# A transformer layer on one core: whole banks for the probabilities, norm scales on VectorE, four more tiles turned by DMA

## The chip, the cores and the metric

The kernel runs on one core of a Trainium2 chip. The metric is the device time of one execution in microseconds, as the median of several. The engines are named as in the profile: PE (TensorE's matmuls) with PEld (its weight loads), DVE (VectorE), ACT (ScalarE), POOL (GpSimd), and SP (SyncE, which issues nearly all DMA transfers here).

## The reference

One pre-norm layer in float32: an attention over a sliding window of 256 tokens, then a gated feed-forward network.

```python
S, D, H, Dh, W, F = 2048, 448, 16, 28, 256, 1792
def A(x):
    q, k, v = split(x @ wqkv)                       # 16 heads of 28
    s = einsum("hqd,hkd->hqk", q, k) * Dh ** -0.5
    s = where((i - j >= 0) & (i - j < W), s, -1e9)  # causal, 256 wide
    return einsum("hqk,hkd->hqd", softmax(s), v).merge_heads() @ wo
def B(x):
    return (gelu_tanh(x @ w_gate) * (x @ w_up)) @ w_down
h  = x + A(layernorm(x))        # (x - mean) / sqrt(var + 1e-5)
h2 = h + B(layernorm(h))
```

## The kernel before

**Precision.** A float32 product is made of products of a rounded "hi" part and a remainder "lo". ACT writes the hi part with a copy (line 452, `to_hi`), DVE or POOL subtract it from the value for the lo part (line 455, `to_lo`). So every operand of a large product costs one ACT and one DVE or POOL instruction beside the matmuls.

**Tiles.** The 2048 tokens are 16 tiles of 128, which make four chunks of 512 tokens. The 16 heads are four groups of four. A block `B` is a chunk and a group; there are 16 blocks.

**The norms.** `layer_norms` (469) takes one or two tiles. DVE forms mean and variance (`bn_stats` 488, `bn_aggr` 490, into `bnmv`); POOL makes the scales `bnve` in up to four instructions: eps is added (476), the power -0.5 taken (477), the product with the mean formed (483), and the sign turned (484). `normalise` (501) then lets ACT write the normed tile `xn` (511). What follows needs the tile transposed. For most tiles of the first norm PE does that with four transposes (516), and ACT and DVE write hi and lo out of the bank. For the tiles in `TURNED` (12 to 15), and for the second norm, `turn` lets DVE transpose 32x32 squares (556), sends them by four DMA transfers on SP to a buffer `xl` (559), and `turned` fetches them back with two transfers into `xT` (568, 570), from where ACT and DVE make hi and lo.

**Attention.** Projections (672 for values, 710 for queries and keys) write banks of PSUM; SP moves rows of queries and keys to their places (720, `k<-k` and `k<-q`, and 723). Scores are formed twice. First queries by keys (819, `bank<-k,q`, a "score fill"): DVE takes each row's maximum (883) into `mx`, transposes it into `mt` (916), and SP writes it as one more row of the queries (921, `q<-mt`). Then keys by queries with that row (819, `bank<-q,k`, 29 rows, a "probability fill"): ACT takes the exponential into `pp` (889), POOL cuts the mask out (895), PE multiplies with the values (971). The drain (1009 on DVE, with an ACT copy ahead) adds two banks and frees one of them; transposes (1010), a reciprocal (1011), products on POOL (996) and the output product (1036) follow, and DVE adds the result to the residual `hres` (1039).

Both kinds of fills work on tiles of 64x64, four banks at a time, 512 columns in each. The columns come from pieces of a block in units of 64. `filled` puts the pieces one after the other and cuts a piece that crosses the end of a bank; a fill has one matmul for each piece, head and half. `excursion` (797) issues a score fill and the probability fill of an earlier block together.

**The feed-forward part.** Seven pairs of weights. The first three are classical products (1284, 1296), the last four use sums of the operands to save products (1497); the down products are 1573, their additions to `hres` 1593 (`out_add`), the last ones 1609. Sums of tokens are made at 1192, 1195 and 1198, sums of weights at 1356, each by DVE or POOL. Sums of results are taken out of banks at 1503, 1504 and 1509. Where a bank is read by nothing else before PE may write it again, a one-element read (`seen`, 1410 on ACT, 1411 on DVE) stands for that.

**What sets the order.** Nothing is ordered by hand. Each operation is given an engine, a cost, a latency, a key and its dependences, and a list scheduler (`Lists.run`, 185) walks time while the program is built: at each step it takes, on the engine that can start first, the operation with the lowest key among those that can start. `PLACE` adds an offset to the keys of named units. Operations with `alts` (one-element reads, weight and token sums, copies) go to the engine that would end first. Each engine runs its instructions in the order in which they were written, so any change of a cost, key or dependence may move everything behind it. The matmuls of the feed-forward part are in a fixed chain.

Of the kernel before, what the change touches and what calls it, by code (L numbers as in the profile page):

```python
# [11 lines left out]
AF = mybir.ActivationFunctionType  # L12
# [74 lines left out]
TURNED = (12, 13, 14, 15)  # L87
# [24 lines left out]
}  # L112

# [22 lines left out]
class Lists:  # L136
# [3 lines left out]
    def __init__(self):  # L140
        self.ops, self.seen, self.open, self.all, self.unit = [], {}, {}, {}, None
# [172 lines left out]
def block_kernel(ctx: ExitStack, tc, x, wqk_in, wv_in, wo_in, gu_in, rest_in, cw_in, down_in, out):  # L314
# [154 lines left out]
    def layer_norms(ts, key, kind):  # L469
# [4 lines left out]
        def ve():  # L474
# [3 lines left out]
            if quick:  # L478
                return
# [1462 lines left out]
```

## Time and profile before

| | |
|---|---|
| median of 3 runs | 687.98 us (687.2 to 688.15) |
| profiled execution | 688.24 us, its span 686.5 us |
| PE busy | 673.7 us, 98% of the span |
| DVE / ACT / POOL busy | 77% / 53% / 32% |
| chain that ended last | PE L1497 22%, PE L1573 14% |

A row of the timeline has the start, the duration, the engine, the line, the operation, the result and its operands, the tile, and how many instructions it stands for; what is in brackets at its end is the idle time of that engine just before it, and what ended that. Rows of one engine overlap, since the next matmul begins before the last has left the array: the distance between two starts is what counts. SPq rows are transfers being issued. A row of a window has the busy time of each engine in it, with the instructions in brackets, then the granted clock of PE.

### The profile page before, as it was taken

What the parts mean: (1) busy time and instruction counts of PE and PEld (TensorE: products, weight loads), DVE (VectorE), ACT (ScalarE), POOL (GpSimd) and SP (SyncE); (2) the same over time, 40 slices, a digit from 0 to 9 for tenths busy, and PEclk for the clock granted to TensorE, in tenths of its full rate; (3) what the DMA queues carried; (4) which work ended last, traced back from release to release, by engine and by line L of the source; (5) the groups of instructions that cost most, each with busy time, mean ns of one, the idle gap of its engine ahead of it and who ended that gap; (6) DMA issues with size and microseconds to landing.
All of it is one profiled execution on the core that took longest, in us unless ns stands there. A gap on an engine that the chain in (4) does not pass through costs nothing. (4 is left out here: it accounts for less than half of the span.)

```text
span 686.5 us, 22714 instructions
## 1 busy us (share of the span) xinstructions
PE 673.7 (98%) x9097; PEld 564.5 (82%) x9097; DVE 526.9 (77%) x1569; ACT 361.7 (53%) x785; POOL 218.2 (32%) x444
## 2 busy tenths in 40 slices
PE   8999999999999999999999999999999999999997
PEld 7877778778877776788877988888889889999886
DVE  8887788787788897169977899767657878877754
ACT  5567656565475555557544474534534545546430
POOL 6245654575555564830501013100001220210000
PEclk9999999999999999999999999999999999999999
DMA  8212121013022363126754875315004644543102
GB/s 309 75 51 48 37 50 36 10 48 69 13 82 61 82 215 112 53 83 156 146 124 108 218 213 149 110 46 162 30 16 131 213 136 134 137 148 87 43 15 108
DMA packets 67082, 69.70 MB, mean 102 GB/s; under 512 B 42528, under 2 KB 55008, under 8 KB 66400
## 3 DMA queue, kind: packets, MB, share of 16 engines
q1 hardware_dynamic: 66832, 68.13, 35.5%
q8 instruction: 71, 1.16, 0.7%
q14 instruction: 35, 0.29, 0.2%
q10 hardware_dynamic: 144, 0.11, 0.0%
HBM read 58.82 MB, written 22.45 MB: 118 GB/s over the span
## 5 line engine op out<-in xcount | busy, mean ns | idle before, releaser
L883 DVE CUSTOM_DVE_ANT_0 mt<-bank,mt 128x192 bf16<-128x192 f32 (+4 forms) x368 | 115.5, 373 | 24.2 <-PE bank L819 23.4
L1497 PE MATMUL bank<-xT,proj 64*128 64x512 f32 x645 | 120.3, 388 | 0.0
L895 POOL TENSOR_SCALAR_AFFINE_SELECT pp<-pp 64x256 f32<-64x256 f32 x240 | 95.3, 415 | 46.9 <-ACT pp L889 41.7
L1497 PE MATMUL bank<-xo,proj 64*128 64x512 f32 x456 | 98.0, 388 | 1.4 <-DVE raw L1509 1.0
L889 ACT ACTIVATE pp<-bank 128x512 f32<-128x512 f32 x152 | 79.4, 599 | 25.2 <-PE bank L819 25.1
L1497 PEld LDWEIGHTS bank<-xT,proj 64*128 64x128 f32 x645 | 81.4, 184 | 8.2
L710 PE MATMUL bank<-xT 128*128 128x512 f32 x308 | 79.6, 402 | 0.1
L1573 PE MATMUL bank<-proj,gh 64*128 64x448 f32 x624 | 74.9, 363 | 0.0
L710 PEld LDWEIGHTS bank<-xT 128*128 128x128 f32 x308 | 55.4, 188 | 15.2 <-ACT pp L889 2.0
L1573 PEld LDWEIGHTS bank<-proj,gh 64*128 64x128 f32 x624 | 62.6, 184 | 6.5 <-ACT e L1410 0.6
L1497 PEld LDWEIGHTS bank<-xo,proj 64*128 64x128 f32 x456 | 60.0, 184 | 7.8 <-DVE raw L1509 1.4
L1497 PE MATMUL bank<-xT,w 64*128 64x512 f32 x276 | 53.6, 389 | 0.0
L1497 PE MATMUL bank<-xo,w 64*128 64x512 f32 x240 | 49.5, 391 | 1.2 <-ACT v L1503 0.9
L819 PE MATMUL bank<-k,q 28*64 28x320 f32 (+4 forms) x1560 | 47.8, 336 | 0.4 <-DVE raw L1009 0.2
L1593 DVE TENSOR_TENSOR hres<-bank,hres 128x448 f32<-128x448 f32 (+1 forms) x85 | 46.9, 608 | 1.0 <-PE bank L1573 1.0
L819 PE MATMUL bank<-q,k 29*64 29x192 f32 (+4 forms) x1664 | 44.6, 328 | 1.4 <-issue 1.4
L819 PEld LDWEIGHTS bank<-q,k 29*64 29x64 f32 x1664 | 30.0, 131 | 17.8 <-issue 10.7
L672 PE MATMUL bank<-proj,xT 128*128 128x448 f32 (+1 forms) x220 | 43.0, 338 | 0.3 <-ACT proj L452 0.3
L1410 ACT ACTIVATE e<-bank 1x1 f32<-1x1 f32 x78 | 12.3, 157 | 54.2 <-PE bank L1573 41.1
L819 PEld LDWEIGHTS bank<-k,q 28*64 28x64 f32 x1560 | 36.0, 131 | 5.2 <-issue 1.5
L672 PEld LDWEIGHTS bank<-proj,xT 128*128 128x128 f32 x220 | 34.8, 189 | 6.2 <-issue 1.8
L1573 PE MATMUL bank<-proj,xT 64*128 64x448 f32 x312 | 38.0, 364 | 1.6 <-DVE e L1411 1.4
(201 smaller groups left out, 1327.7 us busy)
## 6 DMA issues: line engine op xcount, KB each, us to landing
gu<-in_gu_dram SPq DMA_DIRECT2D x18, 480.0 KB
proj<-gu SPq DMA_DIRECT2D x24, 288.0 KB
proj<-down SPq DMA_DIRECT2D x22, 224.0 KB
proj<-gu SPq DMA_DIRECT2D x24, 192.0 KB
hres<-in_x_dram SPq DMA_DIRECT2D x16, 224.0 KB
w<-gu SPq DMA_DIRECT2D x12, 288.0 KB
out_dram<-hres SPq DMA_DIRECT2D x15, 224.0 KB
xT<-xn SPq DMA_DIRECT2D x26, 128.0 KB
```

Of the source, the lines that this page charges most:

```text
L672: op("pe", mm(224 * n), 0.29 if n == 1 else 0.38, key + a / 16, lambda a=a, h=h, wb=wb, xb=xb: nc.tensor.matmul(bank[b.k][:, 0:224 * n], x ...
L710: op("pe", mm(512) + 0.002, 0.403, key, lambda a=a, h=h, wb=wb, xb=xb: nc.tensor.matmul(bank[b.k], wqk[m][:, h, wb, :], xT[:, xb, cc * 128 ...
L819: nc.tensor.matmul(bank[banks[j].k][dst, at:at + 64 * n], w, x, start=True, stop=True, tile_position=(32 * j, 64 * h), skip_group_check=True)
L883: nc.vector.tensor_tensor_reduce(junk[turn_of[0]][:, 0:x], bank[b.k][:, 64 * o:64 * o + x], mask[:, lo:lo + x], 1.0, -BIG, OP.add, OP.max, ...
L889: op("act", 0.065 + width * 0.00088, 0.16 + width * 0.00088, key, lambda: nc.scalar.activation(pp[:, j, at:at + width], bank[b.k][:, 0:wid ...
L895: nc.gpsimd.affine_select(a, a, pattern=[[0, 4], [-cm, 64]], compare_op=op_, fill=0.0, base=0, channel_multiplier=cm)
L1410: ways = {"act": (0.08, 0.17, lambda: nc.scalar.activation(e8[0:1, 0:1], bank[b.k][0:1, 0:1], AF.Copy), False), "dve": (0.07, 0.17, lambda ...
L1497: nc.tensor.matmul(bank[b.k], w, xarea(u.cp, xl, xs, side)[:, xk], start=p in (1, 2, 5) and not k and not t, stop=t == 2, tile_position=(6 ...
L1573: nc.tensor.matmul(bank[banks[q].k][:, 0:D], h[oh][0]()[HALF[x], q * 128:q * 128 + 128], d[wh][0]()[HALF[x]], start=not ph and not y and n ...
L1593: op("dve", 0.07 + w * 0.463 / D, 0.163 + w * 0.463 / D, key, lambda: nc.vector.tensor_tensor(hres[:, t, c0:c0 + w], bank[b.k][:, c0:c0 + ...
```

## The change

- Tiles 8 to 11 of the first norm join `TURNED`: 16 PE transposes go, and four DVE transposes, 16 transfers to DRAM and 8 back come.
- The pieces of the probabilities are laid in another order in blocks from 4 on, and the score tiles of the third chunk too (for the first three groups), so that fewer are cut at a bank's end. Matmuls of the probabilities: 832 before, 736 now; products with the values: 96 fewer; of the scores: 780 before, 772 now. The columns stay as they were.
- The scales of a norm: the eps is added on DVE (for the first four tiles on POOL), the power is taken on POOL, and the negative product with the mean is one DVE instruction that reads POOL's result.
- Of the last down products, the odd quarters of the chunk that is finished last but one are added by an ACT copy into SBUF and a POOL addition instead of a DVE addition.
- The scheduler's cost of a fill grows by 0.03 for each matmul above 23, a case without a choice is caught, operations get names and may be pinned (`HAND`, empty), and `PLACE` has other entries throughout.

```diff
-TURNED = (12, 13, 14, 15)
+TURNED = (8, 9, 10, 11, 12, 13, 14, 15)
...
 PLACE = {
-    "k3": -17.1, "kv0": -31, "ln1.4": 18, "q0.0": 6, "kv1": -72, "v3.0": 77, "ln1.5n": 25, "q0.2": -37, "ln1.10": -54,
+    "k6": 16, "ln1.1": 11, "k1": 24, "ln1.2n": -10, "v1.0": 42, "ln1.4": -36, "q0.0": -108, "kv1": -9, "q0.1": -10,
...
-        def ve():
-            e = bnve[:, :, i:i + n]
-            nc.gpsimd.tensor_scalar(e[:, 0], bnmv[:, i:i + n, 1], EPS, None, op0=OP.add)
-            nc.gpsimd.tensor_tensor(e[:, 1], e[:, 0], nhalf[:, 0:n], op=OP.pow)
-            if quick:
-                return
...
-                nc.gpsimd.tensor_tensor(e[:, 0], bnmv[:, i:i + n, 0], e[:, 1], op=OP.mult)
-                nc.gpsimd.tensor_scalar(e[:, 2], e[:, 0], -1.0, None, op0=OP.mult)
...
+        first = kind == "ln1" and ts[0] < 4
+        cost = 0.3 if first else 0.08
+        op("pool" if first else "dve", cost, cost + 0.09, key(ts[0]), lambda: (nc.gpsimd if first else nc.vector).tensor_scalar(
+            e[:, 0], bnmv[:, i:i + n, 1], EPS, None, op0=OP.add), stats, scales)
+        op("pool", 0.6 + 0.1 * n, 0.65 + 0.1 * n, key(ts[0]), lambda: nc.gpsimd.tensor_tensor(
+            e[:, 1], e[:, 0], nhalf[:, 0:n], op=OP.pow), [*scales, "nhalf"], scales)
+        if not quick:
+            op("dve", 0.08, 0.17, key(ts[0]), lambda: nc.vector.scalar_tensor_tensor(
+                e[:, 2], bnmv[:, i:i + n, 0], -1.0, e[:, 1], op0=OP.mult, op1=OP.mult), [*stats, *scales], scales)
...
-    score_fills = filled([((B, i), len(tile_keys(B, i)[0][0])) for B in range(NB) for i in range(4)])
+    score_fills = filled([((B, i), len(tile_keys(B, i)[0][0])) for B in range(NB)
+                           for i in ((0, 2, 3, 1) if block(B)[1] == 2 and block(B)[0] < NG - 1 else range(4))])
     prob_fills = filled([((B, x), PIECES[x][4]) for B in range(NB) for x in
-                         ("ABdf" if B < 4 else "ABDFCE" if B % 2 == 0 else "CEABDF")])
+                         ("ABdf" if B < 4 else "ACBFED" if B % 2 == 0 else "DACBFE")])
...
-            cost = width * 4 / 2400 + (0.06 if not n and len(steps) > 1 else 0.02)
+            cost = width * 4 / 2400 + (0.06 if not n and len(steps) > 1 else 0.02) + 0.03 * max(0, len(work) - 23)
...
+        aside_ = m == 13 and c and q % 2
+        if aside_:
+            buf, tok = ((VM[6][0], VM[6][1]), (SPARE[2][0], SPARE[2][1]))[q // 2]
+            op("act", 0.47, 0.57, key, lambda: nc.scalar.activation(buf()[:, 0:D], bank[b.k][:, 0:D], AF.Copy), (), [tok], b)
+            op("pool", 1.1, 1.15, key, lambda: nc.gpsimd.tensor_tensor(hres[:, t, :], hres[:, t, :], buf()[:, 0:D], op=OP.add),
+               [h, tok], [h], port=True)
```

The order that results is shown at three places. A row has the line, the operation, the result with its operands, and the tile; line numbers are those of each kernel's own file, where 455 has become 470, 1195 and 1198 have become 1207 and 1210, 1356 is now 1368, 1411 is now 1423, 1509 is now 1521, 559 is now 570, 720 is now 731 and 921 is now 933. The banks 140 to 147 of before are called 144 to 151 after.

First, DVE's queue in the feed-forward part, at the third pair of weights (`w` and `xn` hold a pair's sums of weights). Before:

```order
L1195 TENSOR_TENSOR raw<-raw,xT 64x512
L1356 TENSOR_TENSOR xn<-w_5069,xn 64x384
L1356 TENSOR_TENSOR xn<-w_5069 64x128
L455 TENSOR_TENSOR w_5069<-w_5069 128x384
L455 TENSOR_TENSOR w_5069<-w_5069 128x256
L455 TENSOR_TENSOR w_5069<-xn,w_5069 128x384
L1411 COPY e_74<-bank_145 1x1
```

Now:

```order
L1204 TENSOR_TENSOR raw<-xT 128x512
L1368 TENSOR_TENSOR xn<-w_4865,xn 64x384
L1368 TENSOR_TENSOR xn<-w_4865 64x128
L1423 COPY e_74<-bank_149 1x1
L470 TENSOR_TENSOR w_4865<-w_4865 128x384
L1423 COPY e_74<-bank_151 1x1
L470 TENSOR_TENSOR w_4865<-w_4865 128x256
L470 TENSOR_TENSOR w_4865<-xn,w_4865 128x384
```

The read of the bank (145, now 149) has moved ahead of the three subtractions that write `w`.

Second, DVE's queue where the sums of tokens for the second half are made (`xo`, `xT`, `v`, `e` are buffers of such sums). Before:

```order
L455 TENSOR_TENSOR proj<-proj 128x448
L1192 TENSOR_TENSOR e_5070<-xo 128x512
L1195 TENSOR_TENSOR v<-e_5070,xo 64x512
L455 TENSOR_TENSOR xo<-e_5070,xT 128x512
L455 TENSOR_TENSOR xo<-v,xT 128x512
L1198 TENSOR_TENSOR v<-xT,v 64x512
L1509 TENSOR_TENSOR raw<-bank_141,raw 128x512
L1509 TENSOR_TENSOR e_5071<-bank_143,e_5071 128x512
```

Now:

```order
L470 TENSOR_TENSOR proj<-proj 128x448
L1204 TENSOR_TENSOR e_4866<-xo 128x512
L1207 TENSOR_TENSOR v<-e_4866,xo 64x512
L470 TENSOR_TENSOR xo<-e_4866,xT 128x512
L1521 TENSOR_TENSOR raw<-bank_145,raw 128x512
L1521 TENSOR_TENSOR e_4867<-bank_147,e_4867 128x512
```

The sum of line 1198 is no longer in DVE's queue here, it stands in POOL's, and the subtraction of `v` has moved behind the two reads of banks.

Third, SP's queue around the first row of maxima (`q<-mt`; `xl` and `xT<-xl` are the transfers of turned tiles). Before:

```order
L720 DMA k_157<-q_161 4x512
L1057 DMA raw<-in_wo_dram 128x448
L720 DMA k_157<-q_161 4x512 x3
L921 DMA q_158<-mt 1x4x128 x4
L1057 DMA raw<-in_wo_dram 128x448
L559 DMA xl_136<-xn 32x14x32 x3
L921 DMA q_159<-mt 1x4x128 x4
```

Now:

```order
L570 DMA xl_137<-xn 32x14x32 x4
L731 DMA k_161<-q_165 4x512 x4
L1069 DMA raw<-in_wo_dram 128x448
L579 DMA xT<-xl_137 128x3x128
L581 DMA xT<-xl_137 128x128
L731 DMA k_161<-k_160 4x512
L933 DMA q_162<-mt 1x4x128 x4
L731 DMA k_161<-k_160 4x512 x3
L579 DMA xT<-xl_136 128x3x128
L581 DMA xT<-xl_136 128x128
L1069 DMA raw<-in_wo_dram 128x448
L933 DMA q_163<-mt 1x4x128 x4
```

Transfers of two turned tiles now stand ahead of the first rows of maxima, and the fetch of another between the first and the second.

More of the change, by code (lines that the diff above doesn't have):

```diff
@@ L124 @@
 class Op:
-    __slots__ = ("eng", "cost", "lat", "key", "fn", "deps", "users", "left", "banks", "port", "ready", "start", "fin", "unit",
+    __slots__ = ("eng", "cost", "lat", "key", "fn", "deps", "users", "left", "banks", "port", "ready", "start", "fin", "unit", "name",
                  "size", "tag", "mode", "alts", "then", "soft")
@@ L256, in run @@
                     best = c, e
+            best = best or (choice("pe", False), "pe")
             t, o, got = best[0]
@@ L472, in layer_norms @@
         quick = kind == "ln1" and ts[0] < QUICK
[L474 to L484 removed]
+        e = bnve[:, :, i:i + n]
+        stats, scales = [("bnmv", t % 4) for t in ts], [("bnve", t % 4) for t in ts]
         L.unit = f"{kind}.{ts[0]}"
@@ L491, in layer_norms @@
                [("bnst", t % 2)], [("bnmv", t % 4)])
-        cost = (1.25 if n == 1 else 1.6) - 0.3 * quick
-        op("pool", cost, cost + 0.05, key(ts[0]), ve,
-           [*(("bnmv", t % 4) for t in ts), "nhalf"], [("bnve", t % 4) for t in ts])
+        first = kind == "ln1" and ts[0] < 4
[7 more added lines that the diff above has]
+                e[:, 2], bnmv[:, i:i + n, 0], -1.0, e[:, 1], op0=OP.mult, op1=OP.mult), [*stats, *scales], scales)
         for t in ts:
@@ L1592, in out_add @@
         h = span("h", t + part[0], w / D)
-        op("dve", 0.07 + w * 0.463 / D, 0.163 + w * 0.463 / D, key, lambda: nc.vector.tensor_tensor(
-            hres[:, t, c0:c0 + w], bank[b.k][:, c0:c0 + w], hres[:, t, c0:c0 + w], op=OP.add), [h], [h], b, part=part)
+        aside_ = m == 13 and c and q % 2
[4 more added lines that the diff above has]
+               [h, tok], [h], port=True)
+        else:
+            op("dve", 0.07 + w * 0.463 / D, 0.163 + w * 0.463 / D, key, lambda: nc.vector.tensor_tensor(
+                hres[:, t, c0:c0 + w], bank[b.k][:, c0:c0 + w], hres[:, t, c0:c0 + w], op=OP.add), [h], [h], b, part=part)
         if ORDER2[m][1] not in [c for _, c in ORDER2[m + 1:]]:
```

18 lines of the change are left out of this document (12 added, 6 removed), and 31 rows, old and new, of the table PLACE.

## The prediction

> **What bounds the kernel now.** I read the page's busy shares first, then the windows, the waits of the matmul engine, and the timeline at each wait.
>
> ```profile
> span 686.5 us, 22714 instructions
> PE 673.7 (98%) x9097; PEld 564.5 (82%) x9097; DVE 526.9 (77%) x1569; ACT 361.7 (53%) x785; POOL 218.2 (32%) x444
> ```
>
> PE is idle for only 12.8 us. A change can therefore gain in two ways: shorten PE's own stream, or close a share of these 12.8 us. The windows (columns: us, then busy us of PE, PEld, DVE, ACT and POOL, then the clock) show where the gaps lie and that the clock is full:
>
> ```profile
> 20.00:50.00 30.00, 30.00 (x304) 24.50 (x303) 25.47 (x112) 18.11 (x35) 10.84 (x24) 1.00 0.21 60
> 300.00:350.00 50.00, 48.59 (x500) 40.10 (x486) 46.07 (x89) 33.89 (x75) 12.19 (x13) 1.00 0.54 117
> 400.00:450.00 50.00, 48.27 (x433) 40.68 (x431) 44.41 (x83) 29.24 (x66) 10.07 (x8) 1.00 0.46 136
> 450.00:500.00 50.00, 50.00 (x462) 43.12 (x460) 32.52 (x65) 21.80 (x47) 1.99 (x3) 1.00 0.28 81
> ```
>
> Where DVE is 65% busy (450 to 500) PE never stops; where it is 89 to 92% busy PE loses 1.4 and 1.7 us in 50. So PE bounds the span and DVE's queue makes the gaps. The waits of PE agree (total, times, longest):
>
> ```profile
> PE bank L819 <- issue: 1.6, 2, 1.4
> PE bank L1573 <- DVE e L1411: 1.4, 1, 1.4
> PE bank L1497 <- DVE raw L1509: 1.3, 2, 1.0
> PE bank L1497 <- ACT v L1503: 0.9, 1, 0.9
> ```
>
> The profiled execution took 688.24 us: 686.5 of span and 1.74 around it. The median shown is 687.98, 0.26 lower. I sum against 686.5 and then add 1.74 and take off 0.26.
>
> **Term 1, the transposes.** Tiles 8 to 11 no longer go through PE. Four matmuls fall away for each, priced by the distance from their row to the next on PE:
>
> ```profile
> 29.94 0.60 PE L516 MATMUL bank<-ident,xn 128*128 128x128 f32 x4
> 30.30 0.57 PE L672 MATMUL bank<-proj,xT 128*128 128x224 f32 x3
> ```
>
> 0.36 us for a tile, four tiles: **-1.5 us**, certain if what replaces them is in time (term 7).
>
> **Term 2, the pieces of the scores and probabilities.** The probabilities' matmuls fall from 832 to 736: six fills of 32 become fills of 16 with the same 512 columns in each bank. The scores' fall from 780 to 772: three fills of 32, three of 24, one of 20 and two of 16 become eight of 24 and one of 20. The trace counts two records for each matmul. The first three rows are probabilities, the others scores:
>
> ```profile
> 53.39 1.12 PE L819 MATMUL bank<-q,k 29*64 29x128 f32 x48
> 282.34 1.31 PE L819 MATMUL bank<-q,k 29*64 29x192 f32 x64
> 285.85 1.12 PE L819 MATMUL bank<-q,k 29*64 29x320 f32 x32
> 54.30 1.15 PE L819 MATMUL bank<-k,q 28*64 28x192 f32 x32
> 198.44 1.33 PE L819 MATMUL bank<-k,q 28*64 28x64 f32 x48
> 160.32 1.52 PE L819 MATMUL bank<-k,q 28*64 28x64 f32 x64
> ```
>
> Between 64 and 32 records a fill of probabilities gains 1.31 - 1.12 = 0.19 us: six give 1.1 at most. Where a score fill follows at once it overlaps the end, and the gain may be nothing, so I take **-0.5** (0 to -1.1). The score fills go from 3 x 1.52 + 3 x 1.33 + 2 x 1.15 = 10.85 to 8 x 1.33 = 10.64, the one of 20 left out on both sides; the three full fills could by overlap count for as much as 0.37 each, so I take **-0.5** (-0.2 to -1.1). The products with the values lose as many matmuls, 96. Priced like the 32 extra records above (0.19/32 = 6 ns a record) 192 records are 1.1 us; if columns alone count, nothing. I take **-0.3**, near the low end, since these run as long streams in which each matmul can hide the one before.
>
> The Trainium skill (TensorE: Matmul & The Clock Gate, "Wait — 56ns, not 53.3ns?") says that matmuls never start closer than about 25 ns. Taken for each record, the 400 that go would be worth 10 us, an estimate from that page. The trace disagrees for records: the 48 at 53.39 took 0.91 us to the next row at 54.30, 19 ns each.
>
> **Term 3, the gaps of the second half.** Two are named by the waits. First DVE, then the matmul that waited:
>
> ```profile
> 342.00 0.64 DVE L1195 TENSOR_TENSOR raw<-raw,xT 64x512 f32<-64x512 f32 x1
> 343.46 0.90 DVE L455 TENSOR_TENSOR w<-w 128x384 fp32r<-128x384 f32 x2
> 344.27 0.55 DVE L455 TENSOR_TENSOR w<-xn,w 128x384 fp32r<-128x384 f32 x1
> 344.73 0.14 DVE L1411 COPY e<-bank 1x1 f32<-1x1 f32 x1
> 344.93 1.54 PE L1573 MATMUL bank<-proj,xT 64*128 64x448 f32 x12 [1.38 <-DVE e L1411]
> ```
>
> The one-element read frees a bank, and stood behind the three `w` subtractions. In the changed order it stands ahead of all three, so it can run at about 343.4, 1.3 us earlier: **-1.4**. What is late next are the `w` pieces, weights of a later pair, with more than 1.5 us of PE's stream before them.
>
> ```profile
> 444.66 1.30 POOL L455 TENSOR_TENSOR xo<-xo,xT 128x512 fp32r<-128x512 f32 x1 [8.70 <-ACT xT L452]
> 444.70 1.80 DVE L1198 TENSOR_TENSOR v<-xT,v 64x512 f32<-64x512 f32 x1
> 446.43 0.68 DVE L1509 TENSOR_TENSOR raw<-bank,raw 128x512 f32<-128x512 f32 x1
> 447.16 0.73 PE L1497 MATMUL bank<-xo,proj 64*128 64x512 f32 x3 [1.04 <-DVE raw L1509]
> 401.07 0.68 DVE L1198 TENSOR_TENSOR v<-xT,v 64x512 f32<-64x512 f32 x1
> ```
>
> L1198 took 1.80 us beside a POOL instruction, 0.68 without it. It now goes to POOL and leaves DVE's queue at this place, so L1509 can start some 1.8 us earlier: **-1.0**. What is late next is `v` itself, which ACT rounds into `xT` (L452), for a fill further on. Two gaps of a few tenths follow queues that are shorter in the changed order (near 410 and 417): **-0.5**. Together **-2.9**. The bounds are 0, if new queues cost as much elsewhere, and -6.0, what this part exceeds its steady pitch by.
>
> **Term 4, the gaps of the attention part.** The longest is this one; the three rows ahead of the drain L1009, which frees the bank, are a norm's statistics and two weight subtractions:
>
> ```profile
> 266.16 0.63 DVE L488 BATCH_NORM_STATS2 bnst<-hres 128x6 f32<-128x448 f32 x1
> 266.70 1.15 DVE L455 TENSOR_TENSOR proj<-proj 128x448 fp32r<-128x448 f32 x2
> 267.78 0.68 DVE L1009 TENSOR_TENSOR raw<-bank,oblk 128x512 f32<-128x512 f32 x1
> 268.74 0.45 PE L819 MATMUL bank<-q,k 29*64 29x128 f32 x8 [1.39 <-issue]
> ```
>
> Such meetings are chance of the order. The fills are cut anew and all else is placed anew, so some go and some come: **-1.0**, between 0 and the -4.2 that five such places of this part come to.
>
> **Term 5, the end.** Nine additions follow each other on DVE after the last matmuls begin:
>
> ```profile
> 678.69 4.41 DVE L1593 TENSOR_TENSOR hres<-bank,hres 128x448 f32<-128x448 f32 x9 [0.45 <-PE bank L1573]
> 679.20 2.78 PE L1609 MATMUL bank<-w,gh 128*128 128x448 f32 x15
> ```
>
> PE ends at 681.98, DVE at 683.10, 0.49 us an addition. Two now go by an ACT copy and a POOL addition. Seven leave DVE tied to PE: 681.98 + 0.5 = 682.5, **-0.6**. If POOL's pair of additions (about 1.3 each by the POOL row at 444.66) ends last, nothing is gained; if POOL holds DVE up as at 444.70, it is +0.5. The Trainium skill (SBUF — State Buffer, "Who interferes with whom") has it that VectorE with two SBUF inputs collides with a GpSimd that reads SBUF, with one not. The row at 444.70 agrees for two; these additions read one bank and one SBUF tile, so by the page -0.6 stands.
>
> **Term 6, the scales of the norms.** The reciprocal root stays on POOL, with the eps ahead of it (but for the first tiles) and the last product after it on DVE. DVE now waits for POOL at 16 places:
>
> ```profile
> L477 POOL TENSOR_TENSOR bnve<-bnve 128x2 f32<-128x2 f32 (+1 forms) x17 | 12.7, 747 | 12.7 <-ACT xn L511 11.4
> L895 POOL TENSOR_SCALAR_AFFINE_SELECT pp<-pp 64x256 f32<-64x256 f32 x240 | 95.3, 415 | 46.9 <-ACT pp L889 41.7
> ```
>
> Some eight of the places lie before about 50 us. At the others one or two instructions stand between, 0.1 to 1.3 us against 0.75 (two roots: 1.5) and whatever masks POOL still has, at 0.42 each. Behind the waiting product stand score maxima and bank drains, for which PE waits. Below: nothing. Above: two roots and three masks, 2.7 us, at nine places. I take +0.6 of PE. POOL also loses two instructions a norm, which brings scales earlier. With what other new meetings bring: **+1.0**.
>
> **Term 7, SP's queue.** Tiles 8 to 11 add 16 transfers of transposed rows and 8 back. The prices of an issue are a quarter of each row:
>
> ```profile
> 26.45 2.46 SPq L720 DMA_DIRECT2D k<-k  x4
> 48.13 2.45 SPq L921 DMA_DIRECT2D q<-mt  x4
> 68.42 1.95 SPq L559 DMA_DIRECT2D xl<-xn  x4
> ```
>
> Ahead of the first `q<-mt` (row maxima, without which the first probabilities can't run) now stand 8 `xl` and 2 `xT` more and 4 key copies fewer: 10 x 0.49 - 4 x 0.61 = 2.5 us. It ended at 50.6 and PE used it at 53.39; PE's own work before that point is 1.7 us shorter by the new order and term 1. SP is idle 3.4 us in pieces before 48. So the first fill is late by 2.5 + 1.7 - 2.8 = 1.4 if the idle time can't be used, less if it can; 3.5 if a landing takes as long as the whole slack. I take **+1.0** (0 to 3.5). By the fifth `q<-mt` 16 more issues are 7.8 us, against some 8.8 us of idle.
>
> **Sum.** -1.5 - 0.5 - 0.5 - 0.3 - 2.9 - 1.0 - 0.6 + 1.0 + 1.0 = -5.3. 686.5 - 5.3 + 1.74 - 0.26 = **682.7 us**.
>
> **The rivals.**
>
> *The gaps only move.* PE keeps the fixed terms 1 and 2 (-2.8) and term 5 (-0.6), terms 3 and 4 come back elsewhere, one of the two waits bites (+1): 687.98 - 2.4 = 685.6. For it: DVE is 89 to 92% busy just where the gaps are, and the sum of its work is not smaller. Against it: the two named waits have a single instruction each ahead of them, which the new order moves.
>
> *SP's queue holds the first probabilities* for the whole 3.5 us and again once or twice: the term is +4.7 instead of +1: 686.4. For it: SP issues for nearly all of 22 to 50 us. Against it: later `q<-mt` have margin.
>
> *DVE stands waiting for POOL's root* (slower). Of nine places in the attention part and the first weights each holds the drain or maximum behind it for its 1.5 to 2.7 us, as the two subtractions did at 266.70, where PE lost 1.4. At nine times 0.9, PE loses 8.1 instead of 1: 682.7 + 7.1 = 689.8. It decides when more than 0.7 us a place reaches PE. For it: POOL is the busiest in just this part, and pairs of roots stand together. Against it: PE holds several banks ahead, and most waits of DVE pass unseen.
>
> *Small matmuls cost by number.* At 38 ns a matmul (0.91/24), the 200 that go are worth 7.6 us instead of 1.3: 676.4. Against it: the fill of 64 records took 0.19 us more than that of 32, 12 ns a matmul.
>
> **How the numbers follow.** Forecast 0.50, its own range 679.5 to 685.0; gaps only move 0.18; SP 0.12; DVE waits for POOL 0.13; cost by number 0.07. Less than 0.2%, 1.4 us, can't be told from no change here. Faster: 0.50, two thirds of 0.18, half of 0.12, and 0.07: 0.75. Same: what is left of these two, 0.12. Slower: 0.13. The range leaves out the last two rivals, 0.20: 678.8 to 687.3.
>
> **What would show it.** L516 with 32 records of PE instead of 48; no L819 group over 48 records. Term 3: no wait of PE for the one-element read near 340 nor for `raw` near 445. Term 6: DVE's idle time ahead of the scale product, by POOL, under 1 us a place. Term 7: the idle time of PE before the first probabilities, 0 to 1.5 us. Term 5: the last DVE addition within 0.6 us of PE's end. The prediction is wrong if PE's idle time is not some 2 us smaller, or if its busy time falls by clearly more or less than 2 to 4 us.

## The result and the profile after

The changed kernel takes **679.66 us** (678.54 to 680.05, 4 runs), the kernel before 687.59 us beside it (4 runs): a ratio of 0.9883 with an interval of 0.9866 to 0.9901, 8.0 us faster. The prediction was 682.7 us, 5.3 under the 687.98 it started from. The direction and the range held, the range narrowly: the lower end of the forecast's own range was 679.5. The gain was half as large again as forecast.

The page of after, its first lines:

```profile
span 678.2 us, 21918 instructions
PE 668.4 (99%) x8685; PEld 555.9 (82%) x8685; DVE 531.4 (78%) x1613; ACT 362.9 (54%) x790; POOL 203.3 (30%) x394
```

PE's idle time fell from 12.8 to 9.8 us and its busy time by 5.3 us. The waits of PE in after (total, times, longest):

```profile
PE bank L1890 <- DVE bank L639: 1.6, 1, 1.6
PE bank L527 <- ACT xn L522: 1.0, 1, 1.0
PE bank L1509 <- DVE e L1423: 0.5, 2, 0.4
```

None of the four waits that the prediction quoted is left at over 0.5 us. The windows of after (the same columns as before):

```profile
20.00:50.00 30.00, 30.00 (x299) 24.64 (x299) 25.98 (x124) 17.75 (x35) 6.56 (x8) 1.00 0.33 83
300.00:350.00 50.00, 50.00 (x428) 43.25 (x426) 45.81 (x96) 30.24 (x63) 11.71 (x10) 1.00 0.63 153
350.00:400.00 50.00, 49.46 (x448) 44.48 (x446) 40.57 (x84) 26.29 (x61) 8.23 (x8) 1.00 0.65 169
400.00:450.00 50.00, 50.00 (x456) 42.19 (x456) 40.96 (x76) 26.52 (x59) 7.74 (x7) 1.00 0.40 117
```

From 300 to 350 DVE is as busy as before (45.81 against 46.07), yet PE loses nothing there. So it is not a lighter load of DVE that closed the gaps.

Busy time alone does not say where the 8.3 us of span went, because a short wait hides inside it. A row of before shows this: the ten matmuls behind the wait start 0.53 us after the two ahead of them, which last 0.36, and only 0.17 counts as idle. These twelve take 1.67 us until the next group starts at 412.03, while twelve of the same kind take 1.22 at 414.11 (the next group starts at 415.33): 0.45 us are lost, and 0.17 of them are shown.

```profile
410.36 0.36 PE L1573 MATMUL bank<-proj,xT 64*128 64x448 f32 x2
410.89 1.30 PE L1573 MATMUL bank<-proj,xT 64*128 64x448 f32 x10 [0.17 <-DVE xT L455]
```

So I cut the span at two places that both kernels have on PE: the start of the first group of 42 classical products that has no projections or attention behind it, and the start of the last 15 matmuls. First the timeline of before, whose last 15 start at 679.20, as the prediction shows:

```profile
330.17 1.08 PE L1284 MATMUL bank<-xT,proj 64*128 64x512 f32 x8
```

Then that of after:

```profile
325.66 1.09 PE L1296 MATMUL bank<-xT,proj 64*128 64x512 f32 x8
670.37 1.88 PE L1628 MATMUL bank<-w,gh 128*128 128x448 f32 x8
```

| part of the span | before | after | difference | forecast |
|---|---|---|---|---|
| to the 42 products: norms, attention, first weights | 330.2 | 325.7 | -4.5 | -1.8 (terms 1, 2, 4, 6, 7) |
| from there to the last 15 matmuls | 349.0 | 344.7 | -4.3 | -2.9 (term 3) |
| from there to the end | 7.3 | 7.8 | +0.5 | -0.6 (term 5) |

Each column is one execution. Three kernels further down have before's order in the first part (`pins`, `pins2`, `pins3`), and there it took 328.5 to 330.1 us; three have after's (`no_aside`, `tail`, `scales_pool`), 325.5 to 325.6. The first row's difference is therefore 2.8 to 4.6 us, 3.8 between the means. The second row holds within a few tenths in all of them, but for what the edits there do on purpose.

The windows of the first two parts tell busy from idle time. Before, then after:

```profile
0.00:330.17 330.17, 326.01 (x5945) 257.14 (x5947) 257.42 (x1041) 198.67 (x420) 171.65 (x392) 1.00 0.31 85
330.17:679.20 349.03, 344.89 (x3141) 304.98 (x3137) 265.61 (x521) 163.04 (x366) 46.52 (x53) 1.00 0.41 114
0.00:325.66 325.66, 321.48 (x5532) 247.88 (x5534) 262.08 (x1075) 199.15 (x423) 165.14 (x354) 1.00 0.34 91
325.66:670.37 344.71, 344.17 (x3141) 305.57 (x3137) 266.10 (x533) 163.17 (x368) 35.86 (x38) 1.00 0.42 116
```

In the first part PE's idle time is 4.2 us in both kernels, and its busy time fell by 4.5 us. In the second part its idle time fell from 4.1 to 0.5 us, while DVE's work there stayed the same (265.6 and 266.1 us).

In the second part the groups of matmuls come in the same order in both kernels, so the gain can be followed from group to group. The lead of after is the difference of the two starts, less the 4.51 us that it already had at the 42 products:

| group starts, before | the same group, after | lead of after | what PE waited for on the way, before |
|---|---|---|---|
| 346.31 | 340.41 | 1.4 | one-element read on DVE, at 344.93 |
| 373.49 | 366.62 | 2.4 | `v` of ACT, at 373.49 |
| 423.04 | 415.70 | 2.8 | short waits for DVE, at 410.89 and 418.97 |
| 447.16 | 438.65 | 4.0 | `raw` of DVE, at 447.16 |
| 679.20 | 670.37 | 4.3 | |

The row of the wait for ACT, in before:

```profile
373.49 0.50 PE L1497 MATMUL bank<-xo,w 64*128 64x512 f32 x2 [0.86 <-ACT v L1503]
```

### The profile page after: what moved, and what is told of

The parts are those of the page before. It is cut to its first block, busy times and chain, and to the rows that moved or that the text cites. A ratio compares the mean times of both kernels' runs of the same rounds, so it can differ in the third digit from the quotient of the medians.

```text
span 678.2 us, 21918 instructions
## 1 busy us (share of the span) xinstructions
PE 668.4 (99%) x8685; PEld 555.9 (82%) x8685; DVE 531.4 (78%) x1613; ACT 362.9 (54%) x790; POOL 203.3 (30%) x394
## 4 chain that ended last, share of the span: by engine, by line
PE 88%; DVE 5%; DMA 3%; issue 1%; SPq 1%; ACT 1%; POOL 0%; DVEq 0%; ACTq 0%
PE bank L1509 26%; PE bank L1585 18%; PE bank L831 10%; PE bank L721 9%; PE bank L1296 7%; PE bank L1048 6%; PE bank L983 6%; PE bank L683 4%; PE bank L1308 2%; DVE mt L895 2%; DMA raw<-in_wo_dram 1%; DMA proj<-gu 1%; DMA hres<-in_x_dram 1%; DVE xn L1368 1%; SPq L731 1%
## 5 line engine op out<-in xcount | busy, mean ns | idle before, releaser
L1509 PE MATMUL bank<-xT,proj 64*128 64x512 f32 x645 | 115.6, 389 | 0.0
L1509 PE MATMUL bank<-xo,proj 64*128 64x512 f32 x456 | 92.7, 389 | 0.4 <-DVE e L1423 0.4
L1509 PEld LDWEIGHTS bank<-xT,proj 64*128 64x128 f32 x645 | 73.0, 184 | 9.5 <-ACT raw L1515 0.3
L1585 PE MATMUL bank<-proj,gh 64*128 64x448 f32 x624 | 72.1, 362 | 0.0
L1509 PEld LDWEIGHTS bank<-xo,proj 64*128 64x128 f32 x456 | 55.7, 184 | 6.1 <-DVE e L1423 0.7
L1509 PE MATMUL bank<-xT,w 64*128 64x512 f32 x276 | 50.9, 389 | 0.0
L1509 PE MATMUL bank<-xo,w 64*128 64x512 f32 x240 | 46.4, 390 | 0.2 <-DVE e L1423 0.2
L831 PE MATMUL bank<-q,k 29*64 29x320 f32 (+4 forms) x1472 | 43.7, 350 | 0.2 <-issue 0.2
L831 PEld LDWEIGHTS bank<-q,k 29*64 29x64 f32 x1472 | 27.1, 131 | 18.2 <-issue 7.6
L983 PE MATMUL bank<-pp,v 64*29 64x192 f32 (+4 forms) x1472 | 38.6, 340 | 0.2 <-ACT pp L901 0.2
L1296 PE MATMUL bank<-xT,proj 64*128 64x512 f32 x312 | 37.9, 390 | 0.0
```

The costliest lines, as they stand in the source:

```text
L831: nc.tensor.matmul(bank[banks[j].k][dst, at:at + 64 * n], w, x, start=True, stop=True, tile_position=(32 * j, 64 * h), skip_group_check=True)
L983: nc.tensor.matmul(bank[banks[h].k][32 * j:32 * j + DH + 1, 64 * lo:64 * hi], v[HALF[h], at_v(4 * c - 2 + kh // 2), 4 * g + j, :], pp[HALF ...
L1296: nc.tensor.matmul(bank[banks[side ^ ph].k], cwbuf[n % 4][0]()[HALF[side], o:o + 128], carea(c, xl, j, side), start=not ph and not j and n ...
L1509: nc.tensor.matmul(bank[b.k], w, xarea(u.cp, xl, xs, side)[:, xk], start=p in (1, 2, 5) and not k and not t, stop=t == 2, tile_position=(6 ...
L1585: nc.tensor.matmul(bank[banks[q].k][:, 0:D], h[oh][0]()[HALF[x], q * 128:q * 128 + 128], d[wh][0]()[HALF[x]], start=not ph and not y and n ...
```

## The experiments

Where a number is compared with after, it is by the ratio to the kernel before, which ran beside each: after has 0.9883.

**Do small matmuls cost by number?** `split_d` cuts one piece of the probabilities in two, in the fills and in the products with the values, and keeps every queue's order (a further edit, left out here, leaves the scheduler's costs as they were).

```diff
+    def cut(kh, n):
+        return [(0, n // 2), (n // 2, n - n // 2)] if kh in (8, 3) and n == 4 else [(0, n)]
...
             if probs:
-                return [(j, dst, at, n, keys_of(B, kh, 1)[rows], q_of(B)[rows, 64 * u:64 * (u + n)], h)]
+                return [(j, dst, at + 64 * a, b, keys_of(B, kh, 1)[rows], q_of(B)[rows, 64 * (u + a):64 * (u + a + b)], h)
+                        for a, b in cut(kh, n)]
...
-                        work.append((h, j, kh, lo, u + n, G.at + at + 64 * (lo - u)))
+                        work += [(h, j, kh, lo + a, lo + a + b, G.at + at + 64 * (lo + a - u)) for a, b in cut(kh, u + n - lo)]
```

> The changed kernel with one piece of each block from 4 on (four units wide) cut in two, in the probability fills and in the products with the values: the numbers of matmuls are those of before again (832 and 96 more), the columns and every engine's order stay as after. By the rows of before (64 records 1.31 us, 32 records 1.12): six fills grow by 0 to 0.19 us each and the value products not at all, since their 112 records of before and 96 records of after both take 2.4 to 2.5 us: +0.2 to +1.1, about 680.2. By the theory that small matmuls cost by number (38 ns each, 192 of them): +7.3, about 687.

Measured: 684.42 us, ratio 0.9945 (0.9930 to 0.9960), 4.3 us slower than after. That fits neither number. Two things were wrong with the edit: it added 224 matmuls, not 192, since the piece exists in the first four blocks too, and it put the two halves directly behind each other on the same 64x64 tile.

`split_all` does it with every piece over one unit (`if n > 1` in `cut`):

> The changed kernel with every piece wider than one unit cut in two, in the probability fills and in the value products; columns and order as after. It shows from which number on a fill is bound by its matmuls. By the rows of before nothing is lost up to 48 records and some 0.2 us for each 16 beyond: fills of 64 to 96 records go from 0.92 to 1.1 to 1.6 us, about +10 to +20 us in all with the value products. If columns alone count: +0. If every matmul costs 38 ns: over +40.

Measured: 721.42 us (a single run), 42 more for 1264 more matmuls, twice the most that its rows of before gave. It has the same flaw. It tells only that far smaller pieces would be dear.

`split_d2` mends both, in the fills as shown and in the products with the values alike:

```diff
+    def cut(B, ke, n):
+        return [(0, n // 2), (n // 2, n - n // 2)] if ke == 8 and n == 4 and B > 3 else [(0, n)]
...
-                for j in range(4):
-                    for h, kh, u in ((0, ke, ue), (1, ko, uo)):
-                        work += part(B, h, j, kh, u, n, 64 * o, True)
+                for a, b in cut(B, ke, n):
+                    for j in range(4):
+                        for h, kh, u in ((0, ke, ue), (1, ko, uo)):
+                            work += part(B, h, j, kh, u + a, b, 64 * (o + a), True)
```

> As split_d, but the cut pieces follow each other as whole pieces (in split_d two halves of a piece stood directly behind each other on the same 64x64 tile, and four more blocks were cut), so that the matmuls number 832 and 832 as before, 192 more than after, over the same columns and in the same orders. Term 2 of the prediction: 0.2 to 1.1 us slower than after. By number at the 21 ns that split_d paid for each: 4.1 us slower, 683.7. If split_d's cost came from the order on the tile alone: under 1.5 us.

Measured: 681.49 us, ratio 0.9902 (0.9886 to 0.9918). That is 1.3 us slower than after by the two ratios, whose intervals overlap, and 0.8 in the trace (its first part took 326.4 us). Term 2's 0.2 to 1.1 is the nearest; the 7 us of the rival by number are out, and 4.1 too. An added matmul costs some 7 ns here (1.3 us by 192) and 19 in `split_d`, where consecutive ones share a tile. PE's busy time in the probability fills says the same: 43.7 us in after, 44.6 in `split_d2`, 48.0 in `split_d`.

**Are the two gaps of the second half a matter of DVE's queue?** `pins` is the kernel before, with the pinning of after (`HAND`) and two entries in it: the read of bank 145 and the sum of tokens.

```diff
+HAND = {"None#5": "act", "tx1.0#3": "pool"}
```

> The kernel before with two operations pinned: the one-element read at 344.7 us goes to ACT instead of DVE, the sum of tokens at 444.7 us to POOL instead of DVE; all else is as before. If the two gaps come from DVE's queue as term 3 has it: -1.4 and -1.0, about 685.3, and no wait of PE over 0.5 us near 345 and 447. If gaps only move: the two places are empty but PE waits elsewhere as long, 687.3 or more.

Measured: ratio 0.9989 (0.9976 to 1.0002), no change that can be told. The gap at 447 had shrunk from 1.04 to 0.30, that at 345 had another name. ACT, then PE, of `pins`:

```profile
342.84 1.06 ACT L1320 ACTIVATE v<-bank 128x512 f32<-128x512 f32 x2
343.79 0.14 ACT L1421 ACTIVATE e<-bank 1x1 f32<-1x1 f32 x1
343.99 1.57 PE L1584 MATMUL bank<-proj,xT 64*128 64x448 f32 x12 [1.64 <-ACT e L1421]
```

ACT had no idle time there: its queue stood in the way as DVE's had. `pins2` leaves the read on DVE and writes it ahead of the three subtractions (`ws0#6` to `ws0#8`).

```diff
+HAND = {"tx1.0#3": "pool"}
...
+            if o.name in ("ws0#6", "ws0#7", "ws0#8"):
+                back.append(o.fn)
+            else:
+                o.fn()
+            if o.name == "None#5":
+                [fn() for fn in back]
```

> The kernel before with two places of its order changed and nothing else: the one-element read of 344.7 us stays on DVE but is written ahead of the three subtractions of w, and the sum of tokens of 444.7 us goes to POOL. Pinning that read to ACT had left the gap (1.64 us, now ended by ACT, whose queue was as full). If the place in the queue is the cause: the gap of 1.38 at 345 falls below 0.3 and that of 1.04 at 447 is gone, span about 684.0, time about 2.4 us under before. If PE's own supply (its weights, or the w pieces that are now 0.1 us later) takes the place: under 1.2 us gained.

Measured: ratio 0.9989 (0.9969 to 1.0008). DVE and PE of `pins2`:

```profile
341.78 0.15 DVE L1428 COPY e<-bank 1x1 f32<-1x1 f32 x1
341.96 0.90 DVE L472 TENSOR_TENSOR w<-w 128x384 fp32r<-128x384 f32 x2
343.24 0.68 DVE L1215 TENSOR_TENSOR e<-xo,raw 64x512 f32<-64x512 f32 x1
343.84 0.14 DVE L1428 COPY e<-bank 1x1 f32<-1x1 f32 x1
344.04 0.88 PE L1590 MATMUL bank<-proj,xT 64*128 64x448 f32 x6 [1.18 <-DVE e L1428]
```

The first read ran early and PE went on for half a group of 12. Then it waited for the second read, of the next bank, still behind the subtractions. `pins3` moves both, ahead of the sum of tokens (`tx0.0#17`) too.

```diff
-            if o.name in ("ws0#6", "ws0#7", "ws0#8"):
+            if o.name in ("ws0#6", "ws0#7", "ws0#8", "tx0.0#17") or any(d in back for d in o.deps):
...
-            if o.name == "None#5":
+            if o.name == "None#6":
```

> The kernel before with the sum of tokens of 444.7 us on POOL and with both one-element reads (of banks 145 and 147) written ahead of the three subtractions of w and of the sum of tokens behind them; with the first read alone moved, PE had waited 1.18 us for the second. If these places in DVE's queue are the cause of both gaps: no wait of PE over 0.4 us near 345 and 447, span 2.4 us or more under that of before. If another producer takes over: a wait of about 1 us at 344 to 346 with another name.

Measured: ratio 0.9982 (0.9972 to 0.9993), 1.2 us faster than before (0.5 to 1.9), half of what was expected. PE of before, from the 42 products behind the next group on:

```profile
353.53 4.95 PE L1284 MATMUL bank<-xT,proj 64*128 64x512 f32 x42
358.31 2.60 PE L1573 MATMUL bank<-proj,gh 64*128 64x448 f32 x24
```

PE of `pins3`:

```profile
343.89 1.49 PE L1591 MATMUL bank<-proj,xT 64*128 64x448 f32 x12 [0.44 <-DVE e L1429]
345.21 4.95 PE L1302 MATMUL bank<-xT,proj 64*128 64x512 f32 x42
352.94 5.65 PE L1302 MATMUL bank<-xT,proj 64*128 64x512 f32 x42 [0.34 <-DVE v L1342]
358.20 2.82 PE L1591 MATMUL bank<-proj,gh 64*128 64x448 f32 x24
```

The place in DVE's queue is the cause of the gap at 345: it is down from 1.38 to 0.44, and the 42 products behind it start 1.1 us earlier than in before (345.21 against 346.31). But nearly all of that comes back within 13 us. PE waits 0.34 for `v` of DVE, a wait that before did not have, and the next 42 products take 5.26 us (352.94 to 358.20) against 4.78 in before, so that the 24 behind them start only 0.1 us earlier (358.20 against 358.31). What `pins3` keeps is the gap at 447: there 12 products and the wait behind them take 1.59 us (444.77 to 446.36) against 2.42 in before (444.74 to 447.16), as the sum of tokens is on POOL. That a whole order can keep the gain at 345, after shows: its lead there is 1.4 and stays. It has both reads between the pieces of `w`:

```profile
338.52 0.28 DVE L1368 TENSOR_TENSOR xn<-w 64x128 f32<-64x128 f32 x1
338.84 0.15 DVE L1423 COPY e<-bank 1x1 f32<-1x1 f32 x1
339.01 0.56 DVE L470 TENSOR_TENSOR w<-w 128x384 fp32r<-128x384 f32 x1
339.49 0.14 DVE L1423 COPY e<-bank 1x1 f32<-1x1 f32 x1
```

**What is the table of offsets worth?** `old_place` is the changed kernel with `PLACE` of before.

> The changed kernel with the table of key offsets of before, so that the same operations as after are placed anew. If the gain is half PE's own work (terms 1 and 2, and fewer waits by shorter chains) and half the gaps closed by the order: PE's busy time stays near 668 to 670 and the gaps come back, 683 to 686. If the structural parts bring nearly all: about 680. If the new order brings nearly all: 686 or more.

Measured: 706.25 us, ratio 1.0269 (1.0248 to 1.0291): 27 us slower than after with the same structure, 18 slower than before. Its longest PE wait:

```profile
PE bank L826 <- DVE hres L1046: 6.1, 2, 5.7
```

Two windows of it:

```profile
150.00:200.00 50.00, 42.67 (x751) 33.78 (x741) 28.77 (x124) 22.70 (x48) 19.14 (x45) 0.90 0.22 54
190.00:195.00 5.00, 3.31 (x33) 2.45 (x33) 3.86 (x9) 2.68 (x6) 2.29 (x3) 0.50 0.00 0
```

One wait of 5.7 us, and the clock at 0.50 in the 5 us in which it ends. By its number that is the third case (686 or more), but a kernel 18 us slower than before was in none of the three: a table fitted to one set of operations is not neutral for another. The run therefore does not split the gain into structure and order; it shows that the two can't be told apart by exchanging the table.

**How thin is the cover of the norms' scales?** `root3` takes the power three times in a row; all queues keep their order.

```diff
-        op("pool", 0.6 + 0.1 * n, 0.65 + 0.1 * n, key(ts[0]), lambda: nc.gpsimd.tensor_tensor(
-            e[:, 1], e[:, 0], nhalf[:, 0:n], op=OP.pow), [*scales, "nhalf"], scales)
+        op("pool", 0.6 + 0.1 * n, 0.65 + 0.1 * n, key(ts[0]), lambda: [nc.gpsimd.tensor_tensor(
+            e[:, 1], e[:, 0], nhalf[:, 0:n], op=OP.pow) for _ in range(1 if first else 3)], [*scales, "nhalf"], scales)
```

> The changed kernel with the power on POOL done three times in a row for every norm but the first tiles' (the same value each time), all orders as after: DVE's product finds its input 1.5 us later, 3.1 us later where two norms stand together. If DVE's waits for the root are covered (its idle time ahead of the product was 3.9 us in six places, PE lost none of it): at most 2 us slower than after, 679.5 to 681.5. If each such wait reaches PE through the bank drains behind it: nine places by 1.5 to 3 us, 690 or more.

Measured: 697.64 us, ratio 1.0139 (1.0104 to 1.0174), 17.6 us slower than after for 28 more powers. The rival of the waiting DVE is real, once the wait is longer. Three rows of the timeline of `root3`, DVE and PE:

```profile
284.17 1.95 DVE L504 SCALAR_TENSOR_TENSOR bnve<-bnmv,bnve 128x2 f32<-128x2 f32 x1 [1.47 <-POOL bnve L501]
286.05 0.68 DVE L1516 COPY raw<-bank 128x512 f32<-128x512 f32 x1
286.78 1.21 PE L1308 MATMUL bank<-xT,proj 128*128 128x512 f32 x3 [3.10 <-DVE raw L1516]
```

The window around them:

```profile
285.00:295.00 10.00, 8.22 (x82) 5.55 (x82) 3.63 (x6) 3.51 (x8) 7.15 (x16) 0.83 0.00 0
```

The copy that frees PE's bank stands behind the product that waits for POOL: the chain that the prediction drew. The clock is at 0.83 there. In after DVE's waits for the root (total, times, longest) are short:

```profile
DVE bnve L504 <- POOL bnve L501: 3.9, 6, 1.4
```

`scales_pool` goes the other way: POOL makes the whole scales, as before, in the place of its power, and DVE's two instructions of each norm are gone.

```diff
+        def ve():
+            nc.gpsimd.tensor_scalar(e[:, 0], bnmv[:, i:i + n, 1], EPS, None, op0=OP.add)
+            nc.gpsimd.tensor_tensor(e[:, 1], e[:, 0], nhalf[:, 0:n], op=OP.pow)
+            if quick:
+                return
+            nc.gpsimd.tensor_tensor(e[:, 0], bnmv[:, i:i + n, 0], e[:, 1], op=OP.mult)
+            nc.gpsimd.tensor_scalar(e[:, 2], e[:, 0], -1.0, None, op0=OP.mult)
...
+        op("pool" if first else "dve", cost, cost + 0.09, key(ts[0]), lambda: None, stats, scales)
+        op("pool", 0.6 + 0.1 * n, 0.65 + 0.1 * n, key(ts[0]), ve, [*scales, *stats, "nhalf"], scales)
```

> The changed kernel with the scales of the norms made wholly by POOL as before (for a pair of tiles: eps 0.40, power 0.75, product 0.30, sign 0.26 us in place of the power alone; DVE is rid of its 30 instructions); every other instruction and order as after. By the prediction (the edit costs some +0.6 by DVE's waits): the same or 0.6 faster, 679. If the latency of a norm's scales lies on the path, as three roots in a row cost 18 us for 28 more of them: about 0.6 us lost for each of 13 instances, up to 8 us slower, 683 to 688.

Measured: 679.85 us, ratio 0.9872 (0.9857 to 0.9888): as after, within the intervals, which leave about 1 us open. The trace is sharper: its first part took 325.55 us, that of after 325.66. So the edit of the scales is worth nothing by itself, and its DVE waits cost no more than the longer work on POOL would. About 0.6 us more of latency is covered, 1.5 to 3 us is not.

**How thin is the cover of SP's queue?** `sp_more` sends each of the four transfers of a turned tile of the first norm in two parts.

```diff
-            dma(key, 150, lambda dst=dst, a=a: nc.sync.dma_start(
-                dst, xb()[32 * a:32 * a + 32, 0:D].rearrange("i (b t) -> i b t", t=32)), [at], [("xnd", kind, t, a)], cost=0.53)
+            dma(key, 150, lambda dst=dst, a=a: [nc.sync.dma_start(
+                dst[:, x], xb()[32 * a:32 * a + 32, 0:D].rearrange("i (b t) -> i b t", t=32)[:, x])
+                for x in ((slice(0, 7), slice(7, 14)) if kind == "ln1" else (slice(0, 14),))], [at], [("xnd", kind, t, a)], cost=0.53)
```

> The changed kernel with each of the four transfers of a turned tile of the first norm cut in two, so that SP issues 32 more (0.49 us each, 15.7 us in all by 110 us), 8 of them ahead of the first row of maxima, 13 ahead of the third, 24 ahead of the fifth; all orders as after. In the changed kernel that first row is issued 2.2 us before its use, the third 4.4, the fourth 3.0. If SP's queue stands just within its cover: PE waits for the first probabilities, 2 to 6 us slower than after, 682 to 686. If SP has room: under 1 us.

Measured: 695.26 us, ratio 1.0107 (1.0068 to 1.0147), 15.4 us slower than after. The 32 issues are 15.7 us of SP, about what PE loses, and far more than the 2 to 6 us expected. PE's longest wait is not for a row of maxima but at a turned tile; ACT, DVE and PE of the timeline:

```profile
85.15 0.52 ACT L467 ACTIVATE xT<-xT 128x384 fp32r<-128x384 f32 x1 [3.03 <-DMA xT<-xl]
85.71 0.56 DVE L470 TENSOR_TENSOR xT<-xT 128x384 fp32r<-128x384 f32 x1 [2.39 <-ACT xT L467]
86.97 1.93 PE L832 MATMUL bank<-q,k 29*64 29x320 f32 x28 [2.31 <-DVE mx L896]
```

Three windows from there on:

```profile
86.00:88.00 2.00, 1.03 (x20) 0.52 (x26) 1.15 (x5) 1.96 (x5) 0.00 (x0) 1.00 0.19 32
88.00:90.00 2.00, 2.00 (x54) 1.82 (x44) 1.29 (x3) 1.53 (x5) 0.46 (x1) 0.58 0.12 23
90.00:92.00 2.00, 2.00 (x22) 1.22 (x9) 1.60 (x9) 0.56 (x2) 1.95 (x7) 0.57 0.21 32
```

A late tile holds up DVE's queue, the score maxima stand behind it, and PE waits for the bank. PE's idle time is 6.7 us more than in after (16.5 against 9.8); part of the rest is the clock, at 0.58 and 0.57 in the 4 us behind this wait. So SP's cover is thin behind the change's own 24 issues; how many more would still have been free was not tested.

**What sets the end?** `no_aside` puts all of the last additions back on DVE.

```diff
-        aside_ = m == 13 and c and q % 2
+        aside_ = False
```

> The changed kernel with all of the last additions on DVE again; all before is as after. By term 5 of the prediction: 0.6 us slower than after. If the stores set the end (1.72 MB leave at 360 to 390 GB/s from the first store on, 4.6 us, in both kernels): no difference, within 0.3 us.

Measured: 679.21 us, ratio 0.9868 (0.9836 to 0.9900): the same, but with an interval too wide to tell 0.6 us. In the trace it takes 7.4 us from the start of the last 15 matmuls to the end, no more than after (7.8) and as much as before (7.3). That fits stores which set the end; `tail` tests it. It has this edit and another order of the last down products:

```diff
-            return (0, 0), (1, 1), (0, 1), (1, 0)
+            return (1, 1), (0, 1), (0, 0), (1, 0)
```

> The changed kernel with two edits at its end: all last additions on DVE again, and the last down products in another order, so that the four tiles of one chunk are finished one half (24 matmuls, 2.45 us) earlier. If the stores set the end: they start 2.4 us earlier, the last four tiles' stores (0.9 MB, 2.4 us) then follow PE's end, and the time falls by 0.8 to 1.5 us under after's 679.66, or under no_aside's. If PE and the last addition set it: no difference.

Measured: **678.07 us**, ratio 0.9847 (0.9833 to 0.9860): 2.5 us under after by the ratios, 1.1 to 1.6 by the medians of after and no_aside, and the fastest kernel here. From the start of the last 15 matmuls to the end it takes 6.4 us against 7.4 in `no_aside`, which lacks only the new order. The rates of the DMA queues over the last 16 us (GB/s in 40 slices of 0.4 us), first of after:

```profile
GB/s 0 0 0 0 0 0 0 0 39 0 0 0 0 0 0 0 0 0 0 0 0 4 358 354 380 384 359 384 375 371 359 386 352 256 17 0 0 0 0 0
```

Then of `tail`:

```profile
GB/s 0 0 0 0 0 0 0 0 0 0 0 39 0 0 0 0 0 0 0 30 384 363 384 380 371 249 0 0 0 354 278 388 354 369 371 64 0 0 0 0
```

In after eight tiles leave in one block at 352 to 386 GB/s, so a faster last addition does not shorten it. In `tail` half of them leave while PE still multiplies, and the end comes earlier: the stores set the end.

## Why the prediction was right, and where not

- **Direction and bounds: right.** PE's own stream became shorter and the gaps that DVE's queue made in the second half closed. Of its signs, L527 (516 before) has 32 records instead of 48, no probability fill has more than 48 of its own, and no wait is left near 340 or 445. Three signs did not hold: PE's busy time fell by 5.3 us where 2 to 4 were named, the last DVE addition ended 0.8 us behind PE (673.91 against 673.12) where 0.6 was the bound, and one of the six waits for the root was 1.4 us where each was to stay under 1.
- **Term 3 (-2.9) was too small:** the second half gained 4.3. Its own places came out near their sizes: 1.4 at 345 (forecast 1.4), 1.2 at 447 (1.0) and 0.5 at 410 to 419 (0.5). What it left out is the wait of 0.86 for `v` of ACT at 373.49: the prediction quotes it among PE's waits, at 0.9, and gives it no term. There after gains 1.0 us. That this is due to the change is not shown: the wait came in before and in `pins3` (0.79), but not in `pins` and `pins2`, whose edits lie elsewhere. A second step failed without harm to the sum. "What is late next are the `w` pieces" was wrong: next was the read of the second bank, two places behind, which only after and `pins3` move too. That the two named gaps come from DVE's queue was read rightly; `pins3` shows it for both.
- **Term 4 (-1.0): the reading was wrong.** It held that the fill at 266 waited for the drain at 267.78 behind the norm's statistics. In `pins2` the queues there are those of before and the drain starts at the same 267.78, yet PE has left the fill (265.88) for the next products at 267.37:

```profile
265.88 1.56 PE L836 MATMUL bank<-q,k 29*64 29x128 f32 x48
267.37 0.96 PE L1313 MATMUL bank<-xT,proj 128*128 128x512 f32 x3
267.78 0.68 DVE L1026 TENSOR_TENSOR raw<-bank,oblk 128x512 f32<-128x512 f32 x1
```

  The profile had said "issue", not DVE, and such a gap comes in some executions (1.39 in before, 1.12 in `pins3`) and not in others (`pins2`). What PE waits for then stays open. Nor did gaps close in this part: PE's idle time in it is 4.2 us before and after.
- **Terms 1 and 2 (-1.5, -1.3)** are borne out as far as they were tested. `split_d2` puts the price of the 192 matmuls at 0.8 to 1.3 against 0.8 forecast. The transposes and the score fills were not tested alone. PE's busy time in the first part fell by 4.5, not by 2.8; what the other 1.7 us are stays open, as short waits count as busy time.
- **Terms 6 and 7 (+1.0 each) were not paid.** `scales_pool` shows it for the scales. For SP the first probabilities do: they start with no idle time ahead of them, 2.2 us after the row of maxima was issued. That row went out 1.1 us earlier than before (46.99 against 48.13), not 2.5 later as term 7 added it up: SP's idle time and the new order took up the extra issues. Both causes exist, though, and both are steep: `root3` lost 17.6 us, `sp_more` 15.4. The error was in the cover, which was larger than assumed.
- **Term 5 (-0.6) failed on its cover.** It ended the sum at the last addition and took the stores as following it. SP's issue of the eight stores, 4.12 us from 679.34 on, stood in the trace of before.
- **The rivals.** Gaps that only move: seen at 345 in `pins`, `pins2` and `pins3`, but not at 447, where the gap shrank in all three and nothing came back. In the second half of the change, whose whole order is new, the gaps did not move. In its first part, where PE's idle time is as before, they may have. Cost by number: out. SP's queue and the waiting DVE: true mechanisms, not reached.

The difference of 3.0 us by which the span (-8.3) went beyond the forecast (-5.3) adds up as follows. Terms 4, 6 and 7 forecast 1.0 more idle time in the first part, and there was none: 1.0. PE's busy time there fell by 1.7 more than terms 1 and 2 said. The second half gained 1.4 more, and the end 1.1 less. These are differences of two executions, and the first part alone differs by 1.7 us among the executions with before's order. So that the sum lay within its range is in part luck: the errors had both signs, and the largest has no cause that a run shows.

## What to carry to other kernels

Before a wait is counted as gained, look for the next instruction in the same queue that another engine waits for, and move both; a repair of one place in a full queue can pass the wait on, as at 345. Cover is better measured than estimated: raising a suspected cost with all orders kept showed that two queues, harmless in the undisturbed profile, have little to spare. And follow the end of a kernel to its last transfer, not to its last instruction.

## What the hardware showed beside

- Some waits of PE cost more than their length, because the granted clock falls during or behind them. In `root3` a wait of 1.56 us, soon after others of 0.54 and 0.66, was followed by 3 us at 0.50:

```profile
35.17 2.08 PE L721 MATMUL bank<-xT 128*128 128x512 f32 x4 [1.56 <-DVE mx L895]
35.00:38.00 3.00, 2.83 (x7) 2.26 (x8) 2.91 (x10) 1.52 (x3) 0.00 (x0) 0.50 0.25 43
```

  Behind 2.31 us in `sp_more` it was 0.58 and 0.57 in the next two stretches of 2 us; in the 5 us of `old_place` in which a wait of 5.7 us ended it was 0.50. But 1.53 us in `sp_more` at 69.69 and 1.38 in before at 344.93 left it at 1.00, so the length of one wait does not decide alone. The Trainium skill (TensorE: Matmul & The Clock Gate, "What's actually happening") puts the loss of the clock after an idle window of about 3.4 us; here single waits of 2.31 and of 1.56 us were enough.
- Small matmuls that follow each other on the same 64x64 tile cost more than on changing tiles: the halves of a piece directly behind each other made `split_d` 4.3 us slower for 224 matmuls, in `split_d2` as whole pieces 0.8 to 1.3 us for 192.
- The product of the scales, 0.16 us in the median of after, took 1.95 us in `root3` at 284.17, where POOL ran a mask and a subtraction of two SBUF tiles meanwhile; that these are the cause was not tested.
